# States placed directly behind y, and y and states placed directly ahead of the next scores

## The chip, the cores and the metric

The kernel runs on one core of a Trainium2 chip. The metric is the time of one execution in microseconds (us) on the device, lower is better. A core has a matrix engine (TensorE, in the profile PE for matmuls and PEld for the loads of their stationary operand), a vector engine (VectorE, DVE), a scalar engine (ScalarE, ACT), a general engine (GpSimd, POOL) and a queue engine that issues transfers (SyncE, SP). Each has its own list of instructions, and semaphores tie the lists together.

## What is computed

A gated linear attention runs over four batches of eight heads, 768 tokens and 48 channels, and its result, seen as a matrix of 3072 tokens by 384 columns, goes through a feed-forward block (FFN):

```
for t in range(S):
    state = alpha[:, :, t, :, None] * state + einsum('bhd,bhe->bhde', k[:, :, t], v[:, :, t])
    y[:, :, t] = einsum('bhd,bhde->bhe', q[:, :, t], state)
h = x @ w_in                              # x: 3072 x 384, w_in: 384 x 2048
g = h * (1 / (1 + exp(-h)))               # silu
return g @ w_out                          # w_out: 2048 x 384
```

Everything is in 32-bit floats.

## The kernel before

**Recurrence by chunks.** The sequence is cut into chunks of 128 tokens. There are NT = 24 of them, numbered n; the batch is n mod 4, and the place in the sequence is n // 4, so that four neighbours in the order belong to four different batches and a batch's state is used again four chunks later. The first NA = 8 chunks (the first two of each batch) are prepared in one way, with transposes on TensorE, and the others in another, with transposes on VectorE and through memory. Each chunk passes through stages, which are functions:

- `products` runs the running products of alpha on VectorE (scans L734 and L737's minimum) and makes the scaled keys kp (L745, L749, L751). `quotient` makes the inverse (L762), its scan (L764) and the scaled queries p (L770). `flip` turns the keys (L780) and stores them to memory, `land` reads them back as kn (L790).
- `scores` (L792) multiplies p by kp on TensorE into two banks of PSUM named ps_a. ScalarE copies the result (L812, L818) and POOL masks it (L813, L825). This is called K below.
- `values` (L843) makes y on TensorE: masked scores times v (V below), plus state times queries (Y below), into a ps_a bank. ScalarE copies y to the FFN's input xt (L863).
- `states` (L864) makes the update of the state on TensorE (S below), keys times v, into a ps_a bank, and VectorE adds it to the state (L880).

**FFN by pieces.** Tokens are taken in groups of four chunks. From the second or third group on both products use a block scheme of the Strassen kind, which needs sums of blocks: xc from xt (`combine`, L582 to L587, called in `sums_x`), wx from w_in (`sums_w`), and sums and differences of g (L1033, L1047). A piece of the first product (`enter`, `enter_plain`) is six matmuls of 256 columns into the three ps_m banks; ScalarE and VectorE collect them (L950, L958), and ScalarE applies silu (L923, L955). A piece of the second (`leave`) is eight matmuls of 192 columns into one of two ps_o banks, and there are seven to a half group; VectorE collects them (L1056, L1088, L1099). All matmuls of the FFN use the full 128 x 128 array; V, Y and S use tiles of 32 rows and K tiles of 48 rows. Line L388 is that of the helper which records every matmul.

**The loop.** The main loop (L1203 on) runs over steps, and each step has four slots. A slot first calls its stages and then `fill`, which hands out FFN pieces until the amount that is due at this slot is reached, as long as the chunks which a piece needs have had their y (`bridged`). What is due comes from `marks`, a list of slots, and `phases`, a list of piece numbers. In steps 2 to 7 slot 0 holds the scores of the chunk before, slot 1 the products of the next, slot 2 values and slot 3 states of the chunk before. From step 8 on slot 0 holds `land` and scores, slot 1 products, slot 2 quotient, and slot 3 values, states and flip. Beside these, `audit` has VectorE look over input bits (L697), one look at a time.

**What sets the order.** Once `settle` has run, at about step 8, TensorE keeps the order in which the program calls its matmuls (L381 to L392). Before that, and on the other engines always, a scheduler orders each engine's instructions by its own estimate of when they can run; only the sums of blocks and similar runs are kept in the program's order among themselves. [...] The ps_a pool has three banks, ps_m three and ps_o two.

Of the kernel before, what the change touches and what calls it, by code (L numbers as in the profile page):

```python
# [355 lines left out]
def quotients(  # L356
# [38 lines left out]
    C = 128  # L395
# [6 lines left out]
    NT = B * NCH  # L402
    CH = C // 2
    W = C + 1
    GB = 4
# [26 lines left out]
    def out_bank(i, n):  # L432
        return outs[i].tile([128, 512], F32, name="ps_o")[:, 0:n]

    def ps_attn(n=C):
        return ps_a.tile([128, 512], F32, name="ps_a").rearrange("p (j c) -> p j c", c=n)
# [18 lines left out]
    NA = 2 * GB  # L455
# [133 lines left out]
    def sums_w(pair, upto):  # L589

        r = slice(2 * pair, 2 * pair + 2)
        while sums_done[pair] < min(upto, len(SUMS_W)):
            to, sa, a, sb, b = SUMS_W[sums_done[pair]]
            tc.keep_in_program_order(
                combine(block_w(to)[:, r], sa, block_w(a)[:, r], sb, block_w(b)[:, r]))
            sums_done[pair] += 1
# [246 lines left out]
    def values(n):  # L843
# [17 lines left out]
        if e == 0:  # L861
            xts[half] = xtp.tile([128, NKT, TB], F32, name="xt")
        act.copy(xts[half][:, :, e * C : (e + 1) * C], py[:, 0:NKT])  # L863
    def states(n):  # L864
        c = ctxs.pop(n)
        ci, b, vn = c["ci"], c["b"], c["v"]
        if ci < NCH - 1:

            ps = ps_attn()
            for j in range(NP):  # L870
                for i in range(4):
                    r = slice(32 * i, 32 * i + 32)
                    kn = c["kn"][:, j, r] if n < NA else c["kn"][:, i, 32 * j : 32 * j + 32]
                    pe.matmul(ps[r, j, 0:D], lhsT=kn, rhs=vn[:, 2 * j + i // 2, 0:D],
                              start=True, stop=True)
            for u in range(2):
                r = slice(64 * u, 64 * u + D)
                s, x = st[b][r, :, u, :], ps[r, :, 0:D]
                if ci > 0:
                    dve.tensor_tensor(s, x, s, ALU.add)  # L880
                else:
                    act.copy(s, x)
# [28 lines left out]
    def enter_plain(grp, h, pair):  # L911

        if h == 0:
            g_tiles(grp, pair)
        xt = xts[2 * grp + h]
        for f in range(8 * pair, 8 * pair + 8, 2):
            ps = bank(f // 2 % 3).rearrange("p (e n) -> p e n", e=2)
            for e in range(2):
                for t in range(NKT):
                    pe.matmul(ps[:, e, :], lhsT=w_in[:, t, (f + e) * 128 : (f + e + 1) * 128],  # L920
                              rhs=xt[:, t, :], start=(t == 0), stop=(t == NKT - 1))
            q, i = divmod(f, 4)
            act.activation(gts[grp, h, pair][:, i : i + 2, q % 2, :], ps, AF.Silu)  # L923
            if grp == 1 and pair == h == 0:
                differences(f // 2)
                differences(4 + f // 2)
            if grp > 0 and f % 8 == 6:
                side_by_side(grp, h, pair)
            yield
# [94 lines left out]
    def cells(grp, h, pair, m, k):  # L1024

        return gts[grp, h, pair][:, k::2, :, m * C : (m + 1) * C]
# [8 lines left out]
    def leave(grp, h):  # L1035


        def product(ps, m, k, w, first=False):
            for i in range(HF):
                q = i // 2  # L1040
                x = gts[grp, h, q // 2][:, 2 * (i % 2) + k, q % 2, m * C : (m + 1) * C]
                pe.matmul(ps, lhsT=x, rhs=w[:, i], start=(first and i == 0), stop=(i == HF - 1),
                          skip_group_check=True)

        def subtract(to, x, y):
            for pair in range(NQ // 2):
                dve.tensor_tensor(cells(grp, h, pair, *to), cells(grp, h, pair, *x),  # L1047
                                  cells(grp, h, pair, *y), ALU.subtract)

        def store(m, c, x, y=None):  # L1050
            ci, b = divmod(GB * grp + 2 * h + m, B)
            o = opool.tile([128, HO], F32, name="o")
            if y is None:
                act.copy(o, x)
            else:
                dve.tensor_tensor(o, x, y, ALU.add)  # L1056
            r = b * S + ci * C

            (gps if grp < NG - 1 else nc.sync).dma_start(out[r : r + C, c * HO : (c + 1) * HO], o)  # L1059

        u1, u2, u3, u4 = [rpool.tile([128, HO], F32, name=f"u{j}") for j in range(4)]
        steps = iter(range(7))

        def done():
            if 2 * grp + h in (1, 2):
                sums_w(2 * grp + h - 1, 4 * next(steps) + 4)

        def new(i):
            return out_bank(i, HO)

        a, b = new(0), new(1)
        product(a, 0, 0, b11, True)
        act.copy(u1, a)
        subtract((0, 0), (1, 0), (0, 0))
        done()
        yield
        product(b, 1, 0, t1, True)
        act.copy(u4, b)  # L1078
        done()
        yield  # L1080
        product(a, 0, 1, b21)
        store(0, 0, a)
        subtract((0, 1), (0, 1), (0, 0))
        done()
        yield
        b = new(1)
        product(b, 0, 0, t2, True)
        dve.tensor_tensor(u2, b, u1, ALU.add)  # L1088
        subtract((1, 0), (1, 1), (0, 0))
        dve.tensor_tensor(u2, u2, u4, ALU.add)  # L1090
        done()
        yield
        a = new(0)
        product(a, 0, 1, b22, True)
        store(0, 1, a, u2)
        done()
        yield
        product(b, 1, 0, b12)
        dve.tensor_tensor(u3, b, u1, ALU.add)  # L1099
        store(1, 1, u3, u4)  # L1100
        done()
        yield
        a = new(0)
        product(a, 1, 1, t4, True)
        store(1, 0, a, u3)
        done()
        yield
# [13 lines left out]
    def plain(grp, h, pair):  # L1121
        return (enter_plain(grp, h, pair), 12, 2 * (2 * grp + h) + 2)

    def group(grp):
        return [[(enter(grp, pair), 12, GB * grp + GB)] * 7 for pair in range(2)]

    def output(grp):
        return [[(leave(grp, h), 12, GB * grp + GB)] * 7 for h in range(2)]

    def both(x, y):  # L1130
        for i in range(max(len(x), len(y))):
            pieces.extend(x[i : i + 1] + y[i : i + 1])

    pieces = []
    for h in range(2):
        for pair in range(2):
            pieces += [plain(0, h, pair)] * 4
    pieces += [plain(1, 0, 0)] * 4 + [(leave(0, 0), 12, GB)] * 7
    phases = [len(pieces)]
    pieces += [plain(1, 1, 0)] * 4  # L1140
    both([(leave(0, 1), 12, GB)] * 7, [plain(1, 0, 1)] * 4 + [plain(1, 1, 1)] * 4)
    phases.append(len(pieces))
    before = output(1)
    for grp in range(2, NG):
        sums = sums_x(grp)
# [11 lines left out]

    def go_on():

        nonlocal done  # L1160
        next(pieces[done][0], None)
        done += 1

    audits = audit()
    done, bridged = 0, 0
    STEPS = NT + 1
    SLOTS = 4

    marks = [2 * SLOTS + 2] + [(GB * i + 2 * GB) * SLOTS + 3 for i in range(len(phases))]

    def settle():

# [29 lines left out]

    for step in range(STEPS):  # L1203
        if step == 1:
            load(NIN)
        stages = [[(scores, 1)], [(products, 0)], [(values, 1)], [(states, 1)]]
        if step == 1:

            stages = stages[1::-1] + stages[2:]
        elif step >= NA:  # L1210
            stages = [[(land, 1), (scores, 1)], [(products, 0)], [(quotient, 0)],
                      [(values, 1), (states, 1), (flip, 0)]]
        for slot, group in enumerate(stages):
            for stage, lag in group:
                n = step - lag
                if not 0 <= n < NT:
                    continue
                stage(n)
                if stage is values:
                    bridged = n + 1  # L1220
                if stage is states and n + 1 + NIN < NA:
                    load(n + 1 + NIN)
                if stage is states and n + NV < NT:
                    load_v(n + NV)
            if step * SLOTS + slot == (NA + 1) * SLOTS - 1:
                x = decayed.rearrange("p (o i c) -> p o i c", o=2, c=C)
                for r, o in later:
                    gps.memset(x[r, o, :, 0:CH], 0.0)
            fill(step, slot)
            if step * SLOTS + slot >= NA * SLOTS - 1 and conv_done[1] == NFT and not late:  # L1230
                settle()
    while next(audits, 0) is None:
        go_on()
# [13 lines left out]
    for _ in range(5):  # L1247
        go_on()
    ps = ps_attn()[0:1, 0, 0:1]
# [64 lines left out]
```

## Time and profile before

| | |
|---|---|
| Runs | 557.57, 556.86 and 556.4 us, median 556.86 us |
| Profiled execution | 557.26 us |
| Its span, first to last instruction | 555.5 us |
| Granted clock of TensorE | 0.999 |
| TensorE busy, matmuls | 541.4 us (97%) |
| TensorE busy, loads of the stationary operand | 489.7 us (88%) |
| VectorE busy | 445.4 us (80%) |
| ScalarE busy | 208.5 us (38%) |
| GpSimd busy | 76.1 us (14%) |

A group of instructions is named by its line, engine, operation and tiles, with the tile written first and those read behind the arrow. In a timeline the first number is the start in us from the span's start, the second the length, and a bracket at the end gives the idle time ahead of the instruction and what ended it. Neighbours of one form are put together, with their number behind an x. A matmul in 32-bit floats leaves two records. In the waits, the three numbers are the total in us, how often, and the longest. In the slices each digit is the busy share of a fortieth of the span in tenths.

### The profile page before, as it was taken

The numbers are of one execution on the slowest core, as the hardware profiler recorded it, in microseconds if no ns is written. First come the engines' busy times: TensorE is split into PE (matmuls) and PEld (weight loads), VectorE is DVE, ScalarE is ACT, GpSimd is POOL, SyncE is SP. The second block draws the span as 40 slices with busy tenths as digits, with TensorE's granted clock in tenths as the row PEclk, the third lists the DMA queues.
The fourth block names the chain that finished last, engine by engine and source line by source line (L and its number), as shares of the span: only waits on it lengthen the run. The fifth ranks groups of instructions, "written<-read, shape, count | busy, mean of one in ns | idle before, by whom it ended". The sixth has DMA issues, their size and how long they took to land. (4 is left out here: it accounts for less than half of the span.)

```text
span 555.5 us, 12640 instructions
## 1 busy us (share of the span) xinstructions
PE 541.4 (97%) x5026; PEld 489.7 (88%) x5026; DVE 445.4 (80%) x801; ACT 208.5 (38%) x466; POOL 76.1 (14%) x146
## 2 busy tenths in 40 slices
PE   6999999999999999999999999999999999999996
PEld 4788887998899999899999999988998999999996
DVE  5897788974999899997998986998884796945431
ACT  2556653223333253353353353344263342332100
POOL 3210000222210212021011021021121000001000
PEclk9999999999999999999999999999999999999999
DMA  9998971164454625355545654617642135500000
GB/s 215 246 249 210 232 195 33 47 161 116 117 136 125 159 63 138 86 145 149 139 112 139 193 139 120 191 27 183 170 137 91 54 91 169 172 11 22 10 24 30
DMA packets 99217, 70.09 MB, mean 126 GB/s; under 512 B 56272, under 2 KB 88656, under 8 KB 99152
## 3 DMA queue, kind: packets, MB, share of 16 engines
q1 hardware_dynamic: 97232, 65.30, 45.1%
q0 software_dynamic: 1920, 3.93, 2.0%
q8 instruction: 40, 0.66, 0.5%
q14 instruction: 25, 0.20, 0.1%
HBM read 61.34 MB, written 7.86 MB: 125 GB/s over the span
## 5 line engine op out<-in xcount | busy, mean ns | idle before, releaser
L388 PE MATMUL ps_o<-w_out,g 128*128 128x192 f32 x768 | 134.0, 328 | 0.5 <-DVE o L1056 0.5
L388 PEld LDWEIGHTS ps_o<-w_out,g 128*128 128x128 f32 x768 | 125.6, 190 | 3.5 <-DVE o L1056 1.0
L388 PE MATMUL ps_m<-xt,w_in 128*128 128x256 f32 x480 | 113.6, 383 | 1.5 <-ACT xt L863 1.1
L388 PEld LDWEIGHTS ps_m<-xt,w_in 128*128 128x128 f32 x480 | 89.1, 190 | 14.4 <-ACT xt L863 1.6
L388 PE MATMUL ps_o<-wt,g 128*128 128x192 f32 x576 | 99.7, 326 | 0.0
L388 PEld LDWEIGHTS ps_o<-wt,g 128*128 128x128 f32 x576 | 95.1, 190 | 1.6 <-issue 0.2
L388 PE MATMUL ps_m<-xc,w_in 128*128 128x256 f32 x288 | 70.7, 382 | 0.0
L388 PEld LDWEIGHTS ps_m<-xc,w_in 128*128 128x128 f32 x288 | 53.7, 190 | 7.0 <-DVE g L958 0.3
L1047 DVE TENSOR_TENSOR g<-g 128x512 f32<-128x512 f32 x72 | 50.1, 709 | 8.3 <-PE ps_o L388 8.3
L955 ACT ACTIVATE g<-g 128x1024 f32<-128x1024 f32 x32 | 33.1, 1056 | 61.2 <-DVE g L958 61.1
L1059 POOL DMA_DIRECT2D out_dram<-o x40 | 22.0, 551 | 219.5 <-DVE o L1056 113.7
L825 POOL TENSOR_SCALAR_AFFINE_SELECT g<-g 64x256 f32<-64x256 f32 x64 | 34.9, 546 | 124.4 <-ACT g L818 105.7
L388 PE MATMUL ps_m<-xc,wx 128*128 128x256 f32 x192 | 50.1, 383 | 1.0 <-DVE xc L586 1.0
L950 ACT COPY g<-ps_m 128x512 f32<-128x512 f32 x64 | 36.6, 588 | 37.0 <-PE ps_m L388 36.9
L388 PEld LDWEIGHTS ps_m<-xc,wx 128*128 128x128 f32 x192 | 35.2, 190 | 5.2 <-ACT u L1078 1.2
L958 DVE TENSOR_TENSOR g<-ps_m,g 128x512 f32<-128x512 f32 x56 | 37.1, 683 | 3.2 <-PE ps_m L388 2.7
L734 DVE TENSOR_TENSOR_SCAN u<-al,one 128x516 f32<-128x516 f32 x24 | 29.8, 1240 | 11.9 <-ACT al L731 11.6
L923 ACT ACTIVATE g<-ps_m 128x512 f32<-128x512 f32 x32 | 19.1, 597 | 41.7 <-PE ps_m L388 41.4
L950 ACT COPY part<-ps_m 128x512 f32<-128x512 f32 x32 | 18.9, 590 | 38.0 <-PE ps_m L388 24.0
L697 DVE TENSOR_REDUCE seen<-bits 128x1 f32<-128x512 int32 (+1 forms) x33 | 26.3, 823 | 5.7 <-DMA bits<-in_moe_w_in_dram 5.7
L764 DVE TENSOR_TENSOR_SCAN p<-al,inv 128x516 f32<-128x516 f32 x24 | 29.9, 1247 | 1.0 <-PE ps_a L388 0.3
L1056 DVE TENSOR_TENSOR o<-ps_o,u 128x192 f32<-128x192 f32 x24 | 8.5, 355 | 25.7 <-PE ps_o L388 22.8
(129 smaller groups left out, 648.5 us busy)
## 6 DMA issues: line engine op xcount, KB each, us to landing
bits<-in_moe_w_in_dram SPq DMA_DIRECT2D x24, 512.0 KB, 4.7
bits<-in_moe_w_out_dram SPq DMA_DIRECT2D x16, 384.0 KB, 3.9
at<-in_alpha_dram SPq DMA_DIRECT2D x64, 96.0 KB, 2.5
kt<-in_k_dram SPq DMA_DIRECT2D x64, 96.0 KB, 2.6
qt<-in_q_dram SPq DMA_DIRECT2D x64, 96.0 KB, 2.7
bits<-in_alpha_dram SPq DMA_DIRECT2D x9, 512.0 KB, 4.0
out_dram<-o POOLq DMA_DIRECT2D x40, 96.0 KB, 2.4
flips<-turn SPq DMA_DIRECT2D x12, 256.0 KB, 2.4
```

The costliest lines, as they stand in the source:

```text
L388: in_order(nc.tensor.matmul(*args, **kw))
L697: dve.tensor_reduce(seen[kind][which][:, i : i + 1], x, axis=AX, op=op, apply_absolute_value=True))
L734: dve.tensor_tensor_scan(u[:, end - 1 :: -1], sg[:, end:0:-1], one[:, end:0:-1], 0.0, ALU.mult, ALU.add)
L764: dve.tensor_tensor_scan(p[:, 0:end], sg[:, 0:end], iv[:, 0:end], 0.0, ALU.mult, ALU.add)
L825: gps.affine_select(x, x, pattern=[[0, NP], [1, CH]], compare_op=ALU.is_ge, fill=0.0, base=0, channel_multiplier=-1)
L923: act.activation(gts[grp, h, pair][:, i : i + 2, q % 2, :], ps, AF.Silu)
L950: act.copy(to, ps)
L955: act.activation(x, x, AF.Silu)
L958: dve.tensor_tensor(to, a, b, op)
L1047: dve.tensor_tensor(cells(grp, h, pair, *to), cells(grp, h, pair, *x), cells(grp, h, pair, *y), ALU.subtract)
L1056: dve.tensor_tensor(o, x, y, ALU.add)
L1059: (gps if grp < NG - 1 else nc.sync).dma_start(out[r : r + C, c * HO : (c + 1) * HO], o)
```

## The change

It moves calls and adds no work:

- In steps 2 to 7, values and states stand together in slot 2, so that states come right behind y rather than behind the FFN piece of that slot.
- From the ninth chunk (n = 8) on, values and states wait one step longer (a lag of 2) and stand at the head of slot 0, directly ahead of land and scores of the next chunk. The chunk n = 7 keeps its step; in step 8 values and states stand in slot 3 ahead of flip. The loop gets one step more.
- In this place states write a ps_o bank rather than a ps_a bank. A counter, `left`, of the `leave` pieces handed out says which of the two is empty. Where one or four pieces of a half group are out and the next piece is a `leave` piece too, that piece is handed out ahead of values.
- The marks from the second on move by one slot.

```diff
--- before.py
+++ after.py
@@ -861,12 +861,15 @@
         if e == 0:
             xts[half] = xtp.tile([128, NKT, TB], F32, name="xt")
         act.copy(xts[half][:, :, e * C : (e + 1) * C], py[:, 0:NKT])
-    def states(n):
+    def states(n, behind=False):
         c = ctxs.pop(n)
         ci, b, vn = c["ci"], c["b"], c["v"]
         if ci < NCH - 1:
 
-            ps = ps_attn()
+            if behind:
+                ps = out_bank(0 if left in (3, 4, 5) else 1, 512).rearrange("p (j c) -> p j c", c=C)
+            else:
+                ps = ps_attn()
             for j in range(NP):
                 for i in range(4):
                     r = slice(32 * i, 32 * i + 32)
@@ -1124,8 +1127,14 @@
     def group(grp):
         return [[(enter(grp, pair), 12, GB * grp + GB)] * 7 for pair in range(2)]
 
+    leaves = []
+
+    def last(grp, h):
+        leaves.append(leave(grp, h))
+        return [(leaves[-1], 12, GB * grp + GB)] * 7
+
     def output(grp):
-        return [[(leave(grp, h), 12, GB * grp + GB)] * 7 for h in range(2)]
+        return [last(grp, h) for h in range(2)]
 
     def both(x, y):
         for i in range(max(len(x), len(y))):
@@ -1135,10 +1144,10 @@
     for h in range(2):
         for pair in range(2):
             pieces += [plain(0, h, pair)] * 4
-    pieces += [plain(1, 0, 0)] * 4 + [(leave(0, 0), 12, GB)] * 7
+    pieces += [plain(1, 0, 0)] * 4 + last(0, 0)
     phases = [len(pieces)]
     pieces += [plain(1, 1, 0)] * 4
-    both([(leave(0, 1), 12, GB)] * 7, [plain(1, 0, 1)] * 4 + [plain(1, 1, 1)] * 4)
+    both(last(0, 1), [plain(1, 0, 1)] * 4 + [plain(1, 1, 1)] * 4)
     phases.append(len(pieces))
     before = output(1)
     for grp in range(2, NG):
@@ -1157,16 +1166,18 @@
 
     def go_on():
 
-        nonlocal done
+        nonlocal done, left
+        if pieces[done][0] in leaves:
+            left = left % 7 + 1
         next(pieces[done][0], None)
         done += 1
 
     audits = audit()
-    done, bridged = 0, 0
-    STEPS = NT + 1
+    done, bridged, left = 0, 0, 0
+    STEPS = NT + 2
     SLOTS = 4
 
-    marks = [2 * SLOTS + 2] + [(GB * i + 2 * GB) * SLOTS + 3 for i in range(len(phases))]
+    marks = [2 * SLOTS + 2] + [(GB * i + 2 * GB) * SLOTS + 3 + (i > 0) for i in range(len(phases))]
 
     def settle():
 
@@ -1207,15 +1218,24 @@
         if step == 1:
 
             stages = stages[1::-1] + stages[2:]
+        elif step < NA:
+            stages = stages[0:2] + [stages[2] + stages[3], []]
         elif step >= NA:
-            stages = [[(land, 1), (scores, 1)], [(products, 0)], [(quotient, 0)],
-                      [(values, 1), (states, 1), (flip, 0)]]
+            lag = 2 if step > NA else 1
+            y = [(values, lag), (states, lag)]
+            stages = [[(land, 1), (scores, 1)], [(products, 0)], [(quotient, 0)], [(flip, 0)]]
+            stages[0 if lag == 2 else 3][0:0] = y
         for slot, group in enumerate(stages):
             for stage, lag in group:
                 n = step - lag
-                if not 0 <= n < NT:
+                if not 0 <= n < NT or lag == 2 and n < NA:
                     continue
-                stage(n)
+                if stage is values and lag == 2 and left in (1, 4) and pieces[done][0] in leaves:
+                    go_on()
+                if stage is states:
+                    states(n, lag == 2)
+                else:
+                    stage(n)
                 if stage is values:
                     bridged = n + 1
                 if stage is states and n + 1 + NIN < NA:
```

In the changed kernel the lines from L865 to about L1125 stand three further down (L880 becomes L883, L1047 becomes L1050), and those of the loop 11 to 20 further.

## The prediction

> **What bounds the kernel now.** I read the page's busy times and slices first, then the waits of TensorE, then timelines of TensorE and VectorE where the change cuts in.
>
> ```profile
> PE 541.4 (97%) x5026; PEld 489.7 (88%) x5026; DVE 445.4 (80%) x801; ACT 208.5 (38%) x466; POOL 76.1 (14%) x146
> PE   6999999999999999999999999999999999999996
> ```
>
> TensorE is busy from the second slice to the last but one, so its own order and switches set the time. The chain that ended last is the final store alone and tells nothing.
>
> ```profile
> PE ps_m L388 <- ACT xt L863: 1.1, 4, 0.3
> PE ps_m L388 <- DVE xc L586: 1.0, 1, 1.0
> PE ps_a L388 <- DVE kp L745: 0.5, 1, 0.5
> PE ps_a L388 <- DVE p L770: 0.5, 1, 0.5
> PE ps_m L388 <- DVE g L958: 0.4, 1, 0.4
> ```
>
> In the waits, TensorE loses only some 4 us to other engines after the start. One pass of recurrence work looks so (timeline of TensorE: start, length, operation):
>
> ```profile
> 251.91 1.08 PE L388 MATMUL ps_a<-g,vn 128*32 128x128 f32 x32
> 252.81 0.84 PE L388 MATMUL ps_a<-p,st 128*32 128x128 f32 x24
> 253.47 0.52 PE L388 MATMUL ps_a<-vn,kn 128*32 128x48 f32 x32
> 253.92 1.13 PE L388 MATMUL ps_m<-xc,wx 128*128 128x256 f32 x4
> 254.89 1.89 PE L388 MATMUL ps_m<-xc,w_in 128*128 128x256 f32 x8
> 256.71 0.90 PE L388 MATMUL ps_a<-p,kp 48*64 48x128 f32 x32
> ```
>
> y (V and Y) and states (S) in 32-row tiles, then a piece of FFN, then the scores (K) in 48-row tiles, then FFN again: two excursions from the full array per chunk. From the records' start times I take the cadence: 216 ns a record in ps_m pieces (12 records, 2.6 us), 163 ns in ps_o pieces (16 records, 2.6 us). Entering tiles costs 93 ns over cadence (309 for 216, 256 for 163); leaving costs 136 (S) or 162 (K) ns of interval, and the first full matmul after it takes 104 ns more.
>
> [...] at 139.21 VectorE idled 7.63 us for ScalarE while other chunks' work stood behind. [...]
>
> **The change, part by part.** It adds and removes no instruction: it moves blocks on TensorE, and the scheduler then re-sorts VectorE.
>
> (1) Steps 2 to 7: states join y. Three isolated S blocks (near 42, 76 and 109 us) save about 0.31 each, and three where the last S matmul stood alone (27, 58 and 93 us) about 0.39: 3 x 0.31 + 3 x 0.39 = 2.10. The changed order splits one score block with FFN between, which costs one excursion, 0.35. Early gain 1.75. Bounds 1.2 and 2.1, since S(6) then meets kp (L745) with no slack (0.3).
>
> (2) Chunks 8 to 22: V, Y, S stand directly ahead of K. Each of 15 merges saves one exit and one entry, 136 + 104 + 93 = 333, and adds a change from S to K, which late code does not show. I take 136 (what S to full takes); bounds 43 and 210 (the one early S to K change). So 0.197 us each, 0.12 to 0.29; 15 x 0.197 = 2.96.
>
> (3) y of chunks 8 and 9 comes one piece later; from chunk 10 on K(n+1) comes one piece (2.6 us) earlier. K needs p (L770), VectorE's last product for the chunk. Slack of K behind p in before is 0.15 us at chunk 9 (it stalled), 0.81 at 10, 1.05 at 11, 2.8 and 3.2 at 12 and 13, 4.7 at 14, 4.9 to 14 after. So chunks 9 to 11 are too tight, the later ones hold.
>
> ```profile
> 139.21 0.69 DVE L1033 TENSOR_TENSOR g<-g 128x512 f32<-128x512 f32 x1 [7.63 <-ACT g L923]
> 142.99 0.69 DVE L770 TENSOR_TENSOR p<-turn,p 128x512 f32<-128x512 f32 x1
> 143.83 0.90 PE L388 MATMUL ps_a<-p,kp 48*64 48x128 f32 x32 [0.48 <-DVE p L770]
> ```
>
> K(9) came 4.62 after this L1033. In the changed order two L1047 (0.60 each) and one L584 (0.40) stand between L1033 and L770, 1.6 in all, of which 0.5 fills gaps: +1.1. K(10) came 16.20 after K(9) (143.83, 160.03). Now an L1047 waits for the fourth matmul of a ps_o piece, 10.2 after K(9); behind it to p stand this and another L1047 1.2, kt 1.1, the kp products 0.7, four sums of weights 1.3, qt 1.1, L770 0.7: 16.3, +0.2 with its merge. K(11) came 16.22 after K(10); one piece earlier and merged it is wanted at 16.22 - 2.61 - 0.20 = 13.4. A store addition (L1056) now waits for a ps_o product until 8.9 after K(10); behind it: itself 0.3, four sums 1.45, kt 1.25, kp 0.8, qt 1.15, L770 0.7, so p at 14.55. Stall 1.2, +1.0 after its merge. Sum for these three +2.3, their merges counted. The other 12 merges give 2.36; about 0.3 goes into the wait at 228 us, where L770 now stands ahead of L958: 2.0.
>
> (4) xc. The sums of x for the block scheme (L582 to L587) must be ready for a ps_m product. In before, at chunk 15:
>
> ```profile
> 272.45 1.08 PE L388 MATMUL ps_a<-g,vn 128*32 128x128 f32 x32
> 281.80 0.42 DVE L586 TENSOR_TENSOR xc<-xc,xt 128x256 f32<-128x256 f32 x1
> 283.38 1.03 PE L388 MATMUL ps_m<-xc,wx 128*128 128x256 f32 x4
> 284.27 1.21 DVE L697 TENSOR_REDUCE seen<-bits 128x1 f32<-128x1024 f32 x1
> 286.00 0.68 DVE L1047 TENSOR_TENSOR g<-g 128x512 f32<-128x512 f32 x1
> 286.60 1.12 DVE L708 STREAM_TRANSPOSE turn<-kt 128x512 f32<-128x512 f32 x1
> 288.93 1.11 DVE L708 STREAM_TRANSPOSE turn<-qt 128x512 f32<-128x512 f32 x1
> 290.08 0.69 DVE L770 TENSOR_TENSOR p<-turn,p 128x512 f32<-128x512 f32 x1
> ```
>
> xc was ready 1.2 us ahead of the product. In the changed program the xc sums stand behind that L1047 and L697, woven among the kt and qt transposes. With T the start of V(15), TensorE gives K at T+2.0, ps_o, ps_m, ps_o pieces from 2.84, and wants xc at T+10.75. The L1047 waits for the fourth matmul of the last ps_o piece: 8.14 + 4 x 0.326 = 9.45, or 9.55 with the hand-over. From there, start to start: L1047 0.60, L697 1.13, L582 0.31, kt 0.97, L582 0.31, L749 0.33, L587 0.54, L751 0.34, L584 0.54, qt 1.12, L582 0.34, L770 0.61, L586 0.42 = 7.56. xc at T+17.1: a stall of 6.4 where there was none. It is a loop: TensorE waits for VectorE, which had waited for TensorE's previous piece. VectorE being early cannot shorten it.
>
> ```profile
> 368.38 1.10 PE L388 MATMUL ps_m<-xc,wx 128*128 128x256 f32 x4 [0.96 <-DVE xc L586]
> ```
>
> At chunk 19 the same product stalled 1.13 over cadence in before. In the changed order this xc stands behind chunk 21's second scan (1.15), its kp and p products, two L697 (0.60 each) and an L1047 waiting for the very piece ahead of the product. Added from V(19), xc comes at T+15.3, wanted at T+10.75: 4.5, or 3.4 more than before. If VectorE ran early only the last wait is left, 0.60 + 0.42 behind it: stall 1.3, +0.2; if it starts as late as at 357 us, 7.0, +5.9. I take 3.4. Chunk 11's set has over 4 us to spare.
>
> (5) States in a ps_o bank. The reads (L880) at chunk 15 end at T+4.3, and the next product in that bank starts at T+8.1: hidden by 3.8 us. Without this cover it would cost up to the two additions, 0.7 a chunk. It leaves ps_a's three buffers to y and two score banks. ScalarE (38%), POOL (14%) and the DMA get the same work in another order; the v loads and the flips' stores through SP wait for no less TensorE work than before and have microseconds of room, so I price them at nothing[...].
>
> **Sum.** -1.75 + 2.3 - 2.0 + 6.4 + 3.4 = +8.35. The profiled execution took 557.26 for a span of 555.5, 1.76 around it; the span becomes 563.85, the execution 565.6. The profiled one stands 0.4 above the median 556.86, so I predict 565.2.
>
> **Rivals.** (A) Faster: no wait takes the excursions' place; -1.75 - 2.96 = -4.7, 552.2. For it speaks that TensorE is 97% busy; against, that VectorE is 80% busy with slack under 1.1 us for chunks 9 to 11. It decides if VectorE delivers p and xc no later than TensorE's new order wants them. (B) The stalls at K(9) to K(11) come, the two xc waits don't: -1.75 + 2.3 - 2.0 = -1.45, 555.4. It needs xc ready before T+10.75 at chunk 15, against the order named. (C) One xc wait is small or is made up: with chunk 15 alone +5, with chunk 19 alone +2, so 559 to 562. That states don't leave their place is excluded: the block order on TensorE has moved.
>
> **How the numbers follow.** Forecast 0.55, own range 562 to 568.5 (chunk 19 between +0.2 and +5.9, the S to K change, the early part); C 0.23; B 0.12; A 0.10. About 0.2% (1.1 us) is what a measurement can tell from no change. B straddles it: half of B and A make faster 0.16, half of B same 0.06, the rest slower 0.78. The range from 557 to 568.5 leaves out A, most of B and a little above.
>
> **What would show it.** TensorE's waits name DVE xc L586 at about 6 us at chunk 15 (near 280 us) and 4 us at chunk 19 (near 370), and DVE p L770 three times at 0.2 to 1.7 us; V to K has no ps_m matmul between; the interval from S to K is near 136 ns; isolated S blocks before 115 us are gone. The prediction is wrong if xc L586 is missing from the waits, or if VectorE's order on the chip lets xc finish before the second ps_o piece ends.

## The result and the profile after

The changed kernel takes 570.94 us in the median of five runs (570.15 to 572.96), the kernel before 556.40 beside it: a ratio of 1.0260, with a 95% interval of 1.0247 to 1.0274. The predicted 565.2 has the sign right and is 5.7 us too low; its range ended at 568.5. The profiled execution took 570.83 us for a span of 569.1, so the loss in the span is 13.6 us.

The page of the changed kernel, busy times and two rows of its slices:

```profile
PE 538.9 (95%) x5026; PEld 491.4 (86%) x5026; DVE 446.1 (78%) x801; ACT 209.2 (37%) x466; POOL 75.4 (13%) x146
...
PE   5999999999899999999969999969999999999995
...
PEclk9999999999999999999989999979999999999998
```

The work is the same (5026 matmul records, VectorE's 446 us for 445), but TensorE has two holes, in the slices from 285 and from 370 us, and in both the granted clock falls to tenths of 8 and 7. No slice of before shows either; the clock row of before is

```profile
PEclk9999999999999999999999999999999999999999
```

The waits of TensorE in the changed kernel (total, times, longest):

```profile
PE ps_m L388 <- DVE xc L586: 10.2, 2, 5.8
...
PE ps_a L388 <- DVE p L770: 2.6, 2, 1.6
...
PE ps_m L388 <- DVE w_in L647: 1.3, 1, 1.3
...
PE ps_a L388 <- DVE kp L745: 0.8, 2, 0.5
```

The waits for xc and for p (L770) are those the prediction named. The wait for w_in (L647) it did not have. The two holes in the timeline of TensorE, with the piece behind each:

```profile
289.51 2.04 PE L388 MATMUL ps_m<-xc,wx 128*128 128x256 f32 x4 [5.78 <-DVE xc L586]
291.35 1.53 PE L388 MATMUL ps_m<-xc,w_in 128*128 128x256 f32 x4
292.72 1.03 PE L388 MATMUL ps_m<-xc,wx 128*128 128x256 f32 x4
...
378.64 2.05 PE L388 MATMUL ps_m<-xc,wx 128*128 128x256 f32 x4 [4.41 <-DVE xc L586]
380.48 1.91 PE L388 MATMUL ps_m<-xc,w_in 128*128 128x256 f32 x4
382.19 1.92 PE L388 MATMUL ps_m<-xc,wx 128*128 128x256 f32 x4
```

Four records of 256 columns take 1.03 us when all is well and 1.9 to 2.05 right behind a hole: their starts lie 427 ns apart, not 216. A table by windows of the changed kernel around the first hole (window, its length, TensorE busy with its records, the granted clock as a share of full speed, DMA share, GB/s) says why:

```profile
286.00:289.40 3.40, 0.00 (x0) 0.93 1.05 280
289.40:292.70 3.30, 3.19 (x8) 0.55 0.92 184
292.70:296.00 3.30, 3.30 (x20) 1.00 0.62 171
```

TensorE is granted half its clock from 288.94 to 292.36 us, and all of it afterwards; at chunk 19 it is half from 377.69 to 384.52. Taken over cadence, the hole at chunk 15 is 5.94 us and the slow records behind it cost 1.47 more; at chunk 19 it is 4.57 and 2.97.

VectorE ahead of the first hole, in the timeline of the changed kernel, is the order that the prediction gave:

```profile
282.47 0.69 DVE L1050 TENSOR_TENSOR g<-g 128x512 f32<-128x512 f32 x1
283.08 1.22 DVE L697 TENSOR_REDUCE seen<-bits 128x1 f32<-128x1024 f32 x1
284.21 0.42 DVE L582 TENSOR_TENSOR xc<-xt 128x256 f32<-128x256 f32 x1
...
288.37 0.67 DVE L770 TENSOR_TENSOR p<-turn,p 128x512 f32<-128x512 f32 x1
288.96 0.41 DVE L586 TENSOR_TENSOR xc<-xc,xt 128x256 f32<-128x256 f32 x1
```

L1050 comes first, then the look (L697), and only then the sums, one by one between the transposes, until 289.37. VectorE has no gap over 0.04 us from 274.5 us to there.

**Where the 13.6 us are.** The FFN matmuls come in the same order in both programs, so their records can be set side by side by number. Difference of after against before, in us (the times that end a stage are those of the kernel before):

| Stage | Predicted | Measured |
|---|---|---|
| up to the first FFN matmul | 0 | -1.64 |
| steps 2 to 7, to 128 us | -1.75 | +0.65 |
| K(9) to K(11), to 186 us | +2.3, merges of chunks 8 to 10 in it | +1.80 |
| merges of chunks 11 to 15, to 281 us | -2.0 with those below | -0.62 |
| xc at chunk 15, to 292 us | +6.4 | +7.42 |
| merges of chunks 16 to 18, to 346 us | see above | -0.59 |
| chunk 19, its merge and xc, to 372 us | +3.4 and the merge | +6.15 |
| merges of chunks 20 to 22, and the rest | see above | -0.62 |
| behind the last FFN matmul | 0 | +1.02 |

The first line is chance, no effect to build on: in the eleven kernels profiled here the first FFN matmul started anywhere between 22.6 and 24.6 us. I therefore also use the time from the first to the last start of an FFN matmul, called the FFN stretch below: 526.2 us before, 540.4 after.

### The profile page after: what moved, and what is told of

Same layout as the page of the kernel before. It is cut to its first block, busy times and chain, and to the rows that moved or that the text cites. A ratio compares the mean times of both kernels' runs of the same rounds, so it can differ in the third digit from the quotient of the medians.

```text
span 569.1 us, 12640 instructions
## 1 busy us (share of the span) xinstructions
PE 538.9 (95%) x5026; PEld 491.4 (86%) x5026; DVE 446.1 (78%) x801; ACT 209.2 (37%) x466; POOL 75.4 (13%) x146
## 5 line engine op out<-in xcount | busy, mean ns | idle before, releaser
L388 PE MATMUL ps_m<-xc,wx 128*128 128x256 f32 x192 | 52.8, 400 | 10.2 <-DVE xc L586 10.2
L388 PEld LDWEIGHTS ps_m<-xc,w_in 128*128 128x128 f32 x288 | 55.1, 194 | 7.1 <-DVE g L961 0.3
L1050 DVE TENSOR_TENSOR g<-g 128x512 f32<-128x512 f32 x72 | 48.6, 688 | 12.2 <-PE ps_o L388 12.1
L388 PEld LDWEIGHTS ps_m<-xc,wx 128*128 128x128 f32 x192 | 36.8, 199 | 15.0 <-issue 10.7
L825 POOL TENSOR_SCALAR_AFFINE_SELECT g<-g 64x256 f32<-64x256 f32 x64 | 33.0, 515 | 102.5 <-ACT g L818 87.9
L961 DVE TENSOR_TENSOR g<-ps_m,g 128x512 f32<-128x512 f32 x56 | 37.1, 682 | 4.1 <-PE ps_m L388 3.5
L764 DVE TENSOR_TENSOR_SCAN p<-al,inv 128x516 f32<-128x516 f32 x24 | 30.1, 1256 | 3.4 <-PE ps_a L388 2.9
L388 PE MATMUL ps_a<-g,vn 128*32 128x128 f32 x768 | 27.1, 276 | 1.9 <-POOL g L813 1.7
L697 DVE TENSOR_REDUCE seen<-bits 128x1 f32<-128x512 int32 (+1 forms) x33 | 26.2, 821 | 2.3 <-DMA bits<-in_moe_w_in_dram 2.3
```

The costliest lines, as they stand in the source:

```text
L388: in_order(nc.tensor.matmul(*args, **kw))
L697: dve.tensor_reduce(seen[kind][which][:, i : i + 1], x, axis=AX, op=op, apply_absolute_value=True))
L764: dve.tensor_tensor_scan(p[:, 0:end], sg[:, 0:end], iv[:, 0:end], 0.0, ALU.mult, ALU.add)
L825: gps.affine_select(x, x, pattern=[[0, NP], [1, CH]], compare_op=ALU.is_ge, fill=0.0, base=0, channel_multiplier=-1)
L961: dve.tensor_tensor(to, a, b, op)
```

## The experiments

Three questions were open: why the sums xc stand so late on VectorE, whether the slow records follow from the hole, and what became of the early part.

**The look moved (e1, e6).** In both kernels the looks over the input bits (L697) are handed out in even slots, ahead of the slot's FFN pieces. In the kernel before the last sums xc of a group were called in slot 3, where no look is. The change brings the last y of a group into slot 0, and with it the sums, right behind a look. Chunk 11 has no such wait, and at its step no looks are handed out yet. e1 moves the looks to the odd slots:

```diff
-        if at % 2 == 0 and step > 3 * GB + 2:
+        if at % 2 == 1 and step > 3 * GB + 2:
             next(audits, None)
```

> The changed kernel, with the looks over the input bits (L697) handed out in the odd slots instead of the even ones, so that none is handed out right ahead of the sums xc. In the order VectorE then has, the xc sums stand ahead of the look and of the additions that wait for the ps_o product before. Theory (order): both waits for xc (5.8 and 4.4 us) and the slow matmuls behind them (1.5 and 3.2 us over cadence) go, but for about 1 us at chunk 19 as in the kernel before; 556.5 to 558, from 570.9. Rival (the sums are late because y itself comes a slot later): the waits stay, 568 to 571.

Measured: 558.78 us, 1.0027 times the kernel before (1.0016 to 1.0038), for 1.0260. On that chip the kernel before takes 557.22, so the ratio fits the 556.5 to 558 expected, though the time itself lies 0.8 us above. The FFN stretch falls from 540.4 to 527.1. e6 keeps the looks in the even slots and hands them out behind the pieces:

```diff
-        if at % 2 == 0 and step > 3 * GB + 2:
-            next(audits, None)
         while work_at[done + 1] <= due and pieces[done][2] <= bridged:
             ...
             go_on()
+        if at % 2 == 0 and step > 3 * GB + 2:
+            next(audits, None)
```

> The changed kernel with the looks (L697) in the same even slots, but handed out behind the slot's FFN pieces and sums instead of ahead of them. Theory (what matters is that the look stood ahead of the sums xc in the same slot): as e1, the wait of 5.8 us at chunk 15 gone, at most 1.5 us at chunk 19, no slow records, 557.5 to 559. Rival (e1 gained since the looks were moved elsewhere altogether): waits of 4 us or more, 566 or above.

Measured: 558.47 us, 1.0024 (1.0015 to 1.0033), with an FFN stretch of 526.3. VectorE in its timeline at chunk 15:

```profile
282.33 0.69 DVE L1050 TENSOR_TENSOR g<-g 128x512 f32<-128x512 f32 x1
282.93 0.42 DVE L582 TENSOR_TENSOR xc<-xt,xc 128x256 f32<-128x256 f32 x1
283.27 0.17 DVE L762 RECIPROCAL inv<-least 128x4 f32<-128x4 f32 x1
283.38 0.43 DVE L586 TENSOR_TENSOR xc<-xc,xt 128x256 f32<-128x256 f32 x1
...
287.06 1.21 DVE L697 TENSOR_REDUCE seen<-bits 128x1 f32<-128x1024 f32 x1
```

xc is done at 283.8 and the look comes 3 us later. The sums begin at 278.5, in the changed kernel at 284.21. No wait for xc is left in the waits of e6, one of 0.7 us in those of e1. So it is shown that at chunks 15 and 19 a look called ahead of the sums in the same slot is what makes the sums so late; y being later is not enough. The look alone does not make a wait: in the changed kernel one stands ahead of the sums of chunk 23 too, and there xc is done 2.1 us before its product starts, with no transposes between the sums. Why the scheduler keeps the sums behind the look, whether for the look's transfer in its estimate or for another reason, was not tried.

**The gap filled (e2, e5).** TensorE gets matmuls whose result nobody reads, directly ahead of the product that waits:

```diff
         tt(s[6], s[6], copy(c), ALU.subtract)
         yield
+        if pair == 0 and grp in (3, 4):
+            z = ps_attn(TB)[:, 0]
+            for _ in range((0, 0, 0, 12, 9)[grp]):
+                pe.matmul(z, lhsT=block_w(0)[:, 0], rhs=block_x(grp, 0), start=True, stop=True)
```

> The changed kernel, with 12 matmuls without use (128 x 128 by 256 columns) put on TensorE directly ahead of the product that waits for xc at chunk 15, and 9 at chunk 19. They fill 5.2 and 3.9 us of the two gaps and take nothing from VectorE. Theory (clock): TensorE's clock falls because it stands idle, so with the gaps filled the granted clock stays at 1.0 there, the records behind come every 216 ns and not every 427, and 4.6 us are saved: 566 to 566.5. Rival (the matmuls behind the gap are slow since they share memory with transfers or VectorE, whatever TensorE did before): 570.5 to 571.5 with the same slow records.

Measured: 568.66 us, 1.0211 (1.0194 to 1.0228). Its timeline at chunk 15, and its windows there:

```profile
284.37 5.34 PE L388 MATMUL ps_a<-xt,w_in 128*128 128x256 f32 x24
290.36 1.10 PE L388 MATMUL ps_m<-xc,wx 128*128 128x256 f32 x4 [0.65 <-DVE xc L586]
291.30 1.03 PE L388 MATMUL ps_m<-xc,w_in 128*128 128x256 f32 x4
292.16 1.03 PE L388 MATMUL ps_m<-xc,wx 128*128 128x256 f32 x4
```

```profile
284.30:289.70 5.40, 5.40 (x26) 1.00 0.66 172
290.30:293.30 3.00, 2.94 (x14) 1.00 0.96 206
```

The product still waits for xc until six us behind the piece before, but the clock stays at 1.00 and every record behind it is at full speed, with the DMA as busy (0.96) as beside the records of 427 ns (0.92). So the cause is TensorE's idleness, not what else uses the memory. The total lies between the two ranges expected. The slow records had cost 4.4 us (1.47 and 2.97), not the 4.6 expected, and the FFN stretch falls by 3.6, to 536.8, since at chunk 19 the filling and the wait behind it make 5.4 us where the hole was 4.57.

e5 fills only half (6 and 5 matmuls for 12 and 9):

> As e2, with 6 matmuls without use at chunk 15 and 5 at chunk 19 (2.6 and 2.2 us of work), so that TensorE stands idle for some 3.3 and 2.4 us ahead of the product. In the runs so far idle stretches up to 1.7 us were followed by records at full speed, those of 4.6 and 5.9 us by records of 427 ns. Theory (clock, with a length from which it falls between these): if the slow records appear here, the length is under 2.4 to 3.3 us; if not, it lies between 3.3 and 4.6. Rival (any stretch of waiting costs the same share more): slow records in proportion to the idle time at both places, about 0.8 us each.

Measured: 573.22 us in its one run, span 571.4. Idle stretches of 3.37 and 3.20 us over cadence, and slow records behind both, costing 1.69 and 1.48. So the clock falls behind a hole of 3.2 us already, to records every 427 ns (the filling at chunk 19 left more than the 2.4 I had reckoned). The rival, a loss in proportion, falls: holes of 3.2 to 5.9 us cost 1.5 to 1.7, and once 3.0. But a fixed length does not hold either. In this run the wait for p at K(9), 1.63 us as in the changed kernel, was followed by slow records (1.68 us); in the profiled executions of the changed kernel, e1, e2 and e6 the same wait was followed by none, nor was one of 1.91 us in e4. Without this loss e5's FFN stretch of 541.7 would be 540.0, below the 540.4 of the changed kernel. How an idle stretch lies in time tells more than its length, though not all (1.63 us with 1.56 of it in one step of the clock here, 1.91 with 0.97 in e4); the last section has it.

**The parts alone (e3, e4).** e3 is the kernel before with the early part only:

```diff
+        elif step < NA:
+            stages = stages[0:2] + [stages[2] + stages[3], []]
         elif step >= NA:
```

> The kernel before with only the part for steps 2 to 7: states directly behind y. By the prediction -1.75 us, 554.7. By the trace of the changed kernel -1.0 us, 555.4, with one wait of about 1.5 us near 40 us for the weights' split (L647) that takes part of the gain. Rival (the early part gains nothing outside of chance at the start): 556.4.

Measured: 558.28 us, 1.0016 (1.0008 to 1.0024; the kernel before takes 557.22 there): slower by little, but clear of the noise, and against all three expectations. Its timeline of TensorE:

```profile
38.26 1.08 PE L388 MATMUL ps_a<-g,vn 128*32 128x128 f32 x32
39.16 0.52 PE L388 MATMUL ps_a<-vn,kn 128*32 128x48 f32 x32
39.61 1.13 PE L388 MATMUL ps_m<-xt,w_in 128*128 128x256 f32 x4
42.07 1.13 PE L388 MATMUL ps_m<-xt,w_in 128*128 128x256 f32 x4 [1.33 <-DVE w_in L647]
```

The states do stand behind y, but the next piece waits for a part of w_in that VectorE is still putting together (L645 to L647). VectorE's order around step 3 has moved as well: those operations now come behind the scan L764 and L770 of the chunk. My expectation of -1.0 had taken the earlier start of the changed kernel for a gain of the early part.

e4 is e1 without the early part:

```diff
-        elif step < NA:
-            stages = stages[0:2] + [stages[2] + stages[3], []]
```

> The late part alone (y and states ahead of the next scores from chunk 8 on, in a ps_o bank), with the looks in the odd slots as in e1. Waits for p (L770) at K(9) and K(11) of 1.6 and 1.1 us cost what the merges at 0.2 us each give back: 556.5 to 558, and 0.5 to 1.5 us above e1 because the early part is missing. If merges were worth 0.3 us each: 555.

Measured: 558.70 us, 1.0029 (1.0020 to 1.0039), and no time above e1, as the early part gains nothing. In its trace a merge shows as 0.2 us from chunk 13 on. At chunk 12 0.35 us are lost at the next ps_o product, as in the changed kernel, e1 and e6.

**Keeping what gains (e8, e7, e9).** e8 is e3 with the early part from step 4 on:

```diff
-        elif step < NA:
+        elif 3 < step < NA:
```

> The kernel before with states directly behind y in steps 4 to 7 only. Theory (the early part's loss in e3 is the one wait for the split of w_in, L647, near 41 us, which comes from moving the states of step 3): that wait is gone, and the joins left give 0.8 to 1.0 us: 0.8 below the kernel before, 2 below e3 in the time from the first to the last FFN matmul. Rival: the wait comes anyway, or the split scores cost what the joins give; within 0.2% of the kernel before or above it.

Measured: 556.44 us, 0.9984 (0.9976 to 0.9991), 0.8 us below the kernel before as expected. The theory and its rival both allow this total; the trace decides, as the wait for L647 is gone from its waits. The FFN stretch is 525.9, 1.6 below e3 where 2 was expected, and only 0.3 below before.

e7 is e8 with the late part from chunk 12 and the looks in odd slots. Beside e1 with e8's line it has:

```diff
-            lag = 2 if step > NA else 1
+            lag = 2 if step > NA + GB else 1
...
-                if not 0 <= n < NT or lag == 2 and n < NA:
+                if not 0 <= n < NT or lag == 2 and n < NA + GB:
...
-    marks = [2 * SLOTS + 2] + [(GB * i + 2 * GB) * SLOTS + 3 + (i > 0) for i in range(len(phases))]
+    marks = [2 * SLOTS + 2] + [(GB * i + 2 * GB) * SLOTS + 3 + (i > 1) for i in range(len(phases))]
```

> A version made to keep gains and leave out losses: looks in odd slots, y and states ahead of the next scores only from chunk 12 on (the marks shifted from the third on), states behind y only from step 4 on. Waits for p at K(9) and K(11) as in the kernel before (0.5 and none). 11 merges at 0.2 us give 2.2, the early part about 0.9, less a wait of S(12) for the ps_o bank of up to 1.3 us, a wait for xc at chunk 15 of up to 0.6, and an end that is 1.0 us later in all kernels with the late part: 0.5 to 1.5 us below the kernel before. If the end's 1.0 us and S(12) take all: no difference.

Measured: 555.36 us, 0.9964 (0.9954 to 0.9973), 1.9 us below the kernel before, more than expected, though the FFN stretch of the profiled execution (525.6) is only 0.6 below that of before. The waits for p are back to the one of 0.5 us. Its timeline shows what is left on the table:

```profile
215.95 0.34 DVE L1059 TENSOR_TENSOR o<-ps_o,u 128x192 f32<-128x192 f32 x1
216.35 0.55 PE L388 MATMUL ps_o<-vn,kn 128*32 128x48 f32 x32 [1.98 <-DVE o L1059]
...
217.96 2.07 PE L388 MATMUL ps_m<-xc,wx 128*128 128x256 f32 x4
```

The bank for the states of chunk 12 is not yet empty: a store addition stands behind a scan on VectorE and has still to read it. The wait is 2.16 us over cadence, and slow records follow (1.6 us, those of K among them). The profiled execution is one of the slower ones: its mean clock is 0.994, as in two others of the 16 (0.994 and 0.995), while the remaining 13 have 0.997 or 0.998. So most executions of e7 had less time at half clock than this trace. e9 starts the late part one chunk later, at 13:

```diff
-            lag = 2 if step > NA + GB else 1
+            lag = 2 if step > 13 else 1
...
-                if not 0 <= n < NT or lag == 2 and n < NA + GB:
+                if not 0 <= n < NT or lag == 2 and n < 13:
```

> As e7, but the late part begins at chunk 13. In e7 the states of chunk 12 waited 2.1 us for the ps_o bank, since a store addition (L1059) still had to read it, and slow records behind this wait cost 1.45 more. Theory: both go, one merge of 0.2 is lost, so 3.4 us below e7 in the time from the first to the last FFN matmul (522.2 from 525.6), and 2.5 to 3.5 us below the kernel before in the runs, a ratio of 0.994 to 0.9955. Rival: states of chunk 13 meet the same bank, a wait of about 2 us at 233 us, and the result stays at e7's 0.996.

Measured: 554.50 us, 0.9950 (0.9937 to 0.9963), the lowest here, 2.6 us below the kernel before, with an FFN stretch of 522.7 for 526.2 before. The stretch is 2.9 below that of e7's profiled execution, the median of the runs only 0.9, and the two intervals overlap, so that e9 beats e7 is likely and not shown. Its waits of TensorE:

```profile
...
PE ps_m L388 <- DVE g L961: 1.4, 1, 1.4
PE ps_m L388 <- ACT xt L863: 1.1, 4, 0.3
PE ps_a L388 <- DVE kp L745: 0.8, 2, 0.5
...
PE ps_a L388 <- DVE p L770: 0.5, 1, 0.5
```

The states of chunk 13 meet no full bank. Of the late part's price one wait is left, for L961 at 228 us, 1.4 us for 0.4 before. The stretch is 0.5 us above the one expected (522.2).

## Why the prediction was wrong in size

**Right: the merges, (2).** S to K takes 136 ns in the changed kernel, the value taken; a merge shows as 0.2 us, for 0.197 predicted. That this switch costs what the one from S to the full array costs was an assumption, and it fell right. The total of twelve merges, about -2.0 as forecast, is luck in part: the 0.3 foreseen for the wait at 228 us did not come (0.4 as before), and 0.35 were lost at chunk 12 instead, see (5).

**Right: K(9) to K(11), (3).** The waits over cadence were 1.63, 0.21 and 1.11 us, and the stage lost 1.80, for 2.3. That they come from moving y at chunks 8 to 10 is confirmed by e7 and e9, which leave these chunks alone and have only the wait of 0.5 us of before.

**Right in place and length: the two waits for xc, (4).** 5.94 us at chunk 15, for 6.4. 4.57 at chunk 19, for 4.5, against 1.13 before. The prediction read the order that causes them; which line of the change brings it about, the look in slot 0, it did not find. Its loop, with VectorE held back at L1050 by the ps_o piece, is not shown: the piece's fourth matmul ends at 282.4 us, just when VectorE comes free for L1050, and VectorE had not been idle in the 8 us before. Its order and its load are enough to explain the stall.

**The step that failed** is the term of (4), and of the sum, that prices a stall at its length. "xc at T+17.1: a stall of 6.4 where there was none" left out that TensorE comes back at half its clock: 1.47 and 2.97 us, 4.4 together. Behind both holes the records came every 427 ns for 216, with the granted clock at half for 3.41 and 6.83 us. The kernel before had no stall that could show this: past its start no wait of TensorE is longer than 1.13 us over cadence. The last section has how much idleness went with the loss: 1.98 us or more within one step of the clock, and once 1.56, were followed by half clock here.

**Wrong: the early part, (1).** -1.75 became +0.65 in the stage up to 128 us, 2.4 us off. It priced switches of TensorE alone and never asked what stands ahead of w_in's operations on VectorE when the states of step 3 move. That wait is 1.49 us over cadence; e8, which has the joins of steps 4 to 7 without it, gains 0.3 us in the FFN stretch. Where the other 0.9 of the 2.4 went was not traced. The wait for kp at S(6), given as up to 0.3, was 0.44.

**Not in the sum: the end.** Each kernel with the late part ends 1.0 us later behind its last FFN matmul (6.1 us for 5.1). The last store lands 3.2 us behind that matmul in the kernel before and in the changed one, but SP's closing waits begin 3.8 us behind it for 1.7; the reason was not tried.

**Held in the main: the states in ps_o, (5).** In the changed kernel no wait of TensorE of 0.2 us or more names the state additions (L883). At chunk 12 the cover seems to be missing, though: the additions end at 215.32 us, the next ps_o product starts at 215.47, and it comes 0.35 us over cadence. That it waited for them is not shown. e7 shows the other side of a ps_o bank, one that is still to be read when the states want it, and the price: a wait of 2.16 us and 1.6 us of slow records behind it.

Together, from the predicted +8.35: +4.44 for the clock, +2.40 for the early part, +1.02 for the end and -1.64 for the start make 14.6; the span lost 13.6. The rest is (3) and the xc wait at chunk 15, each 0.5 too high. The start is chance: without it the miss would have been larger. Rivals A and B fell, since all the waits named came, and C, since neither wait for xc was small.

## What to carry to other kernels

In these runs each stall of TensorE of 2.16 to 5.94 us cost its length and 1.5 to 3.0 us of slow records behind it, one or two steps of half clock. A stall of 1.63 us cost 1.68 us more in e5, and nothing more in four other profiles, nor did one of 1.91 us in e4. Price a long stall with such a term, and leave the term open for one near these lengths. When blocks move on an engine that keeps its order, read the new order of every other engine: for each wait, look what the awaited operation itself waits for, and whether that lies just ahead of the waiting one. A call beside the moved one that seems to have nothing to do with it, here a look over input bits in even slots, can decide the order.

## What the runs showed of the hardware

In the trace of the changed kernel the granted clock is either full or half, and the stretches between two of its changes are 279.89, 3.41, 85.33, 6.83 and 180.91 us: 82, 1, 25, 2 and 53 times 3.413 us. A length of 3.41 us is called a step of the clock here. The table has idle stretches of TensorE, the largest part of each that lay within one step, how long the clock was half afterwards, and what the slow records (427 for 216 ns) lost, all in us; the first and the last column are over cadence.

| Idle | Where | Of it in one step | Half clock | Lost |
|---|---|---|---|---|
| 5.94 | changed kernel, chunk 15 | 3.41 | 3.41 | 1.47 |
| 4.57 | changed kernel, chunk 19 | 3.41 | 6.83 | 2.97 |
| 3.37 | e5, chunk 15 | 2.51 | 3.41 | 1.69 |
| 3.20 | e5, chunk 19 | 2.48 | 3.41 | 1.48 |
| 2.16 | e7, chunk 12 | 1.98 | 3.41 | 1.6 |
| 1.63 | K(9), in e5 | 1.56 | 3.41 | 1.68 |
| 1.63 | K(9), in the changed kernel, e1, e6 | 1.54 to 1.56 | 0 | 0 |
| 1.63 | K(9), in e2 | 1.13 | 0 | 0 |
| 1.91 | K(9), in e4 | 0.97 | 0 | 0 |
| 1.54 | e9, at 228 us | 1.37 | 0 | 0 |
| 1.49 | e2, chunk 19, behind the filling | 1.32 | 0 | 0 |

In this table the idleness within one step tells more than the length of the stretch. Every stretch with 1.98 us of it or more was followed by half clock. Of the four profiles with 1.54 to 1.56 us of it at K(9) one was. The beginning of the hole at chunk 15, 1.79 us within the step ahead of the 3.41, was followed by a step at full clock, and so were all rows with less than 1.54 us. The wait of 1.91 us in e4 was cut in two by the end of a step, 0.97 us its larger part, and passed without loss.

The loss did not grow with the stretch: one step of half clock cost 1.47 to 1.69 us, close to the half of 3.41. It was 1.69 at chunk 15 of e5, where TensorE was at work again when the step began, and 1.47 at chunk 15 of the changed kernel, where it began with 0.57 us of idleness. At chunk 19 of the changed kernel the step of half clock began with 0.95 us of idleness and a second one followed, which was not so at chunk 15. In e5 at chunk 15 four records came at full speed, in 0.96 us, before those of 427 ns began. What tips the steps with 1.54 to 1.98 us was not tried.
